# Laying out the start of a three-stage kernel part by part, and moving the second stretch of retention two dense steps later

## The chip, the cores and the metric

One core of a Trainium2 chip runs the whole program in one launch. The metric is the device time of one execution in microseconds (us); less is better. A profile is one execution of the program as the hardware profiler saw it, and times inside it count from the start of its span.

## The reference

Three stages follow each other on 2304 tokens (4 sequences of 576) of width 512:

```python
# 1 retention, 8 heads of width 64
ret = (q @ k.T) / sqrt(64) * gamma[h] ** (i - j) * (i >= j);  x = ret @ v
# 2 a dense layer pair, weights w_in (512 x 2048), w_out (2048 x 512), stored as 64-bit floats
h = x @ w_in;  g = max(h, 0) + log1p(exp(-abs(h)));  x = g @ w_out
# 3 eight experts, the two best per token, weights w1 (512 x 1024), w2 (1024 x 512) each
noisy = x @ w_gate + log1p(exp(x @ w_noise)) * noise
out[token] = sum over its 2 experts of weight * (max(x @ w1[e], 0) @ w2[e])
```

## The kernel before, in words

Values that need more than float16 are kept as a high and a low float16 part, and a product is three matmuls (high-high, high-low, low-high) into one PSUM sum.

**Retention** works on 18 chunks of 128 tokens. Per chunk c: two loads (`qk`, `kv`, 512 KB each, L208 and L212), a scaling of v (`att_scale`, L222), a first stretch on TensorE (`att_in`, L239 and L244), a mask (L246) and the state sums (L257, L259) on VectorE, a second stretch on TensorE (`att_out`, L274), a scaling by position (L282, VectorE) and the split into high (L288, ScalarE) and low (L290). Three chunks make one dense tile of 384 tokens. The tiles in PSUM called `pa` have two buffers; `att_in` takes both, and from chunk 3 on `att_out` takes both.

**The dense layers** go over 6 tiles of 384 tokens by 16 blocks of 128 hidden units. A step `g1(t, f)` is 12 matmuls of 384 columns (L301), then ScalarE and VectorE work on pairs of blocks: Relu and Abs (L310, L311), Exp and Ln (L313, L314), the sum (L315), its high part (L316) and low part (L318). A step `g2(t, f)` is 9 matmuls of 512 columns (L332) and needs the pair that holds block f. The second layer runs four or five steps behind the first.

**The dense weights** arrive as 64-bit floats, 1 MB a piece, 16 pieces, through a ring of 4 buffers. A piece is scaled (L144, ScalarE), and per half its low bits are taken out (L155, ScalarE) and joined with the rest (L156 and L158, VectorE); then its high part (L164, ScalarE) and low part (L165, GpSimd) are made. After the last piece the same buffers take the expert weights, which 64 times are loaded (L347, L349), split (L356 ScalarE, L357 VectorE) and stored as float16 (L361).

**Experts** follow after the dense layers (L678, L706): they begin near 390 us and are not touched.

**What sets the order.** Until the list `order` of dense steps takes over, a string `START` names the parts in the order in which they are traced: `A` load a chunk, `S` scale, `Q` first stretch, `V` second stretch with all that follows, `L`, `a`, `b` load, decode and split a piece, `g` the next dense step, `W` warming matmuls. The scheduler of the framework then arranges every engine's queue itself from this order, and may put later instructions ahead where it thinks an engine free. From chunk 7 on, `at(...)` binds a chunk's parts to dense steps. All loads and stores are issued by SyncE in one queue, in its order; four special transfers are in it too: the routing table, the noise, two small gate weights (L385 to L389), and a write of zeros over the whole 4608 KB output (`out_zero`, L376), which is bound to dense step 44 but has no input to wait for.

Of the kernel before, what the change touches and what calls it, by code (L numbers as in the profile page):

```python
# [10 lines left out]
F32 = mybir.dt.float32  # L11
# [11 lines left out]
P = 128  # L23
C = 128
# [60 lines left out]
def body(ctx, tc, ins, out):  # L85
# [44 lines left out]
    def decode_load(src):  # L130
        d = ring("d64", 0, 0, [1024], I64, 4)
        nc.sync.dma_start(out=d.rearrange("p (a b) -> p a b", a=src.shape[1]), in_=src)
        return d

    def decode(d, k):

        w = d.bitcast(I32).rearrange("p (n t) -> p n t", t=2)
        u = d.bitcast(U16).rearrange("p (n t) -> p n t", t=4)  # L140
        h = d.bitcast(F32).rearrange("p (n t) -> p n t", t=2)[:, :, 1]
        f = ring("df", 1, 0, [1024], F32, 3)
        A = f.bitcast(I32)
        nc.scalar.activation(h, h, AF.Copy, scale=2.0 ** -111)  # L144


        for n in range(2):
            r = slice(n * 512, (n + 1) * 512)
            if n and k < 5:
                low = ps.tile([P, 512], I32, tag="p2", name="low", bufs=3)  # L150
            elif n and k > 6:
                low = ps1.tile([P, 512], I32, tag="pa", name="low", bufs=2)
            else:
                low = ps.tile([P, 512], I32, tag="sm", name="low", bufs=1)
            nc.scalar.activation(low, u[:, r, 1], AF.Copy, bias=2.0 ** -14 - 0.5, scale=2.0 ** -13)  # L155
            nc.vector.scalar_tensor_tensor(out=low, in0=w[:, r, 1], scalar=3, in1=low,  # L156
                                           op0=ALU.logical_shift_left, op1=ALU.bitwise_or)
            nc.vector.scalar_tensor_tensor(out=A[:, r], in0=w[:, r, 1], scalar=-2 ** 31, in1=low,  # L158
                                           op0=ALU.bitwise_and, op1=ALU.bitwise_or)
        return f  # L160

    def parts(f, hi, lo):
        fv = f.rearrange("p (a b) -> p a b", a=hi.shape[1])
        nc.scalar.activation(hi, fv, AF.Copy)  # L164
        nc.gpsimd.tensor_tensor(out=lo, in0=fv, in1=hi, op=ALU.subtract)  # L165

    w_in = ins["moe_w_in"].rearrange("(k p) f -> p k f", p=P)
    w_out = ins["moe_w_out"].rearrange("(c p) d -> p c d", p=P)
    DEC = {}


    PIECES = [("i", 0), ("i", 1)] + [p for i in range(6) for p in (("i", i + 2), ("o", i))] + [("o", 6), ("o", 7)]
    LOADS, DECS, PARTS = list(PIECES), list(PIECES), list(PIECES)

    def piece(what):
        if what == "L" and LOADS:
            w, i = LOADS.pop(0)
            DEC[w, i] = decode_load(w_in[:, :, i * 256:(i + 1) * 256] if w == "i" else w_out[:, 2 * i:2 * i + 2, :])
        elif what == "a" and DECS:
            n = DECS.pop(0)  # L180
            DEC[n] = decode(DEC[n], len(PIECES) - 1 - len(DECS))
        elif what == "b" and PARTS:
            w, i = PARTS.pop(0)
            f = DEC.pop((w, i))
            if w == "i":
                parts(f, wi[:, 0, :, i * 256:(i + 1) * 256], wi[:, 1, :, i * 256:(i + 1) * 256])
            else:
                parts(f, wo[0][:, 2 * i:2 * i + 2, :], wo[1][:, 2 * i:2 * i + 2, :])
# [13 lines left out]

    def kinds(c):
        return [(2 * c + x) % PAIR for x in range(2)]

    def att_load(c):
        qk = ap.tile([P, 2, 8, HALF], F32, name="qk", bufs=3)
        nc.sync.dma_start(out=qk, in_=ins["qk"][c])  # L208
        if c == 0:
            nc.sync.dma_start(out=cd, in_=ins["c_down"])  # L210
        kv = ap.tile([P, 2, 8, D], F32, name="kv", bufs=3)
        nc.sync.dma_start(out=kv, in_=ins["kv"][c])  # L212
        if c < 5:
            n = 2 * c
            m = min(n + 2, PAIR)
            nc.sync.dma_start(out=UP[:, n:m], in_=ins["c_up"][:, n:m])
        LD[c] = (qk, kv)

    def att_scale(c):
        qk, kv = LD[c]  # L220
        e = nc.vector if c < 1 else nc.gpsimd
        e.tensor_tensor(out=kv[:, 1], in0=kv[:, 1], in1=down[:, c % PAIR, :, None].to_broadcast([P, 8, D]), op=ALU.mult)  # L222

    def att_in(c, tag="pa"):

        qk, kv = LD[c]
        ka, kb = kinds(c)
        pool, n = (ps, 3) if tag == "p2" else (ps1, 2)
        pa = pool.tile([P, 8, HALF], F32, tag=tag, name="pa", bufs=n)
        pst = pool.tile([P, 8, D], F32, tag=tag, name="pst", bufs=n)  # L230
        use = (ka < PAIR - 1, kb < PAIR - 1)
        with ExitStack() as tied:
            for j in range(4):
                for r in range(2):
                    g = r * 4 + j
                    for p in range(2):
                        x = p ^ r
# [7 lines left out]
        a = AA[c] = ap.tile([P, 8, HALF], F32, name="a", bufs=2)
        nc.vector.tensor_tensor(out=a, in0=pa, in1=tri[:, None, :].to_broadcast([P, 8, HALF]), op=ALU.mult)  # L246
        sa = ST.get(2 * c)
        for x in range(2):
            if not use[x]:
                continue  # L250
            st = ST[2 * c + x + 1] = ring(("st", x), 1, 21504 + x * 2048, [4, D], F32, 2)
            old = ST.get(2 * c + x)
            for r in range(2):
                y = ROW[1 - r ^ x]
                add = pst[y, 4 * x:4 * x + 4]
                if (ka, kb)[x] == 0:
                    nc.vector.tensor_copy(st[y], add)  # L257
                else:
                    nc.vector.tensor_tensor(out=st[y], in0=old[ROW[r ^ x]], in1=add, op=ALU.add)  # L259

    def att_out(c, tag="pa"):
# [7 lines left out]
        with ExitStack() as tied:  # L269
            both = parts + mine if kk[1] else mine + parts  # L270
            end = {(x, r): n for n, (i, j, x, r) in enumerate(both)}
            for n, (inter, j, x, r) in enumerate(both):
# [16 lines left out]
        e = nc.vector if c < 3 else nc.gpsimd
        e.tensor_tensor(out=lo, in0=f, in1=hi, op=ALU.subtract)  # L290
# [452 lines left out]
    def at(g, f, *a):  # L743
        todo.setdefault(g, []).append((f, a))
# [179 lines left out]
```

## Time and profile before

| | us |
|---|---|
| three runs | 918.84, 920.08, 920.14 (median 920.08) |
| the profiled execution: time / span | 919.36 / 917.5 |
| busy in it: TensorE / VectorE / ScalarE / GpSimd | 878.6 / 668.8 / 383.7 / 256.1 |

How to read it: PE is TensorE's matmuls, DVE VectorE, ACT ScalarE, POOL GpSimd, SP SyncE, whose queue is SPq. The share of busy time is a mean over stages: the first 125 us, the dense stage up to about 390 us and the experts after it have different limits. The profiled time is 0.72 us under the median of the runs.

### The profile page before, as it was taken

What the parts mean: (1) busy time and instruction counts of PE and PEld (TensorE: products, weight loads), DVE (VectorE), ACT (ScalarE), POOL (GpSimd) and SP (SyncE); (2) the same over time, 40 slices, a digit from 0 to 9 for tenths busy, and PEclk for the clock granted to TensorE, in tenths of its full rate; (3) what the DMA queues carried; (4) which work ended last, traced back from release to release, by engine and by line L of the source; (5) the groups of instructions that cost most, each with busy time, mean ns of one, the idle gap of its engine ahead of it and who ended that gap; (6) DMA issues with size and microseconds to landing.
All of it is one profiled execution on the core that took longest, in us unless ns stands there. A gap on an engine that the chain in (4) does not pass through costs nothing. (4 is left out here: it accounts for less than half of the span.)

```text
span 917.5 us, 19458 instructions
## 1 busy us (share of the span) xinstructions
PE 878.6 (96%) x6458; PEld 450.7 (49%) x6458; DVE 668.8 (73%) x1402; ACT 383.7 (42%) x595; POOL 256.1 (28%) x232
## 2 busy tenths in 40 slices
PE   7878999999999999899999999999999999999996
PEld 6544555555455555455544444444444444444442
DVE  5678977797787976334636789878888788887880
ACT  3679966675666674335431122221122212222120
POOL 2366642511311120200412422322223222321112
PEclk8789999999999999999999999999999999999999
DMA  9867999999999994002277664866357746866412
GB/s 349 310 241 224 337 306 406 333 326 371 353 354 330 347 374 102 2 1 69 63 243 141 123 123 82 253 167 173 71 152 174 196 136 163 244 172 162 116 24 34
DMA packets 141103, 186.88 MB, mean 204 GB/s; under 512 B 79888, under 2 KB 89360, under 8 KB 138960
## 3 DMA queue, kind: packets, MB, share of 16 engines
q1 hardware_dynamic: 130512, 164.56, 55.5%
q0 software_dynamic: 10496, 21.05, 11.8%
q8 instruction: 60, 0.98, 0.4%
q14 instruction: 35, 0.29, 0.1%
HBM read 245.67 MB, written 54.20 MB: 327 GB/s over the span
## 5 line engine op out<-in xcount | busy, mean ns | idle before, releaser
L697 DVE STREAM_TRANSPOSE ht<-hr 32x256 f32<-32x256 f32 x608 | 265.1, 436 | 11.7
L678 PE MATMUL ph<-w,xt 128*128 x984 | 220.6, 381 | 2.0 <-DMA xt<-xr 2.0
L706 PE MATMUL py<-w,ht 128*128 x984 | 218.6, 379 | 0.0
L332 PE MATMUL p<-w,g 128*128 128x512 f16 x864 | 204.9, 384 | 7.7 <-POOL w L165 5.3
L301 PE MATMUL pg<-x,wi 128*128 128x384 f16 x1152 | 204.7, 328 | 1.8 <-ACT x L288 1.3
L678 PEld LDWEIGHTS <-xt 128*128 128x128 f16 x984 | 96.5, 98 | 119.0 <-issue 2.2
L301 PEld LDWEIGHTS <-wi 128*128 128x128 f16 x1152 | 111.9, 98 | 85.6 <-issue 2.9
L706 PEld LDWEIGHTS <-ht 128*128 128x128 f16 x984 | 96.3, 98 | 116.1
L718 POOL DMA_INDIRECT out_dram<-y,ti x41 | 64.9, 1583 | 282.0 <-ACT y L717 256.5
L332 PEld LDWEIGHTS <-g 128*128 128x128 f16 x864 | 83.2, 99 | 99.8 <-issue 11.5
L683 ACT ACTIVATE hr<-ph 128x512 f16<-128x512 f32 x82 | 60.1, 733 | 159.3 <-PE ph L678 156.2
L357 DVE SCALAR_TENSOR_TENSOR w<-w 128x1024 f16<-128x1024 f32 x64 | 83.8, 1320 | 36.7 <-ACT w L356 31.2
L684 DVE SCALAR_TENSOR_TENSOR hr<-ph,hr 128x512 f16<-128x512 f32 x82 | 59.4, 728 | 67.7 <-ACT hr L683 66.0
L717 ACT ACTIVATE y<-py,ti 128x512 f32<-128x512 f32 x41 | 28.2, 687 | 180.4 <-PE py L706 175.9
L356 ACT ACTIVATE w<-w 128x1024 f16<-128x1024 f32 x64 | 67.4, 1054 | 62.4 <-DMA w<-in_moe_w_dram 39.3
L315 DVE SCALAR_TENSOR_TENSOR r<-a,r 128x768 f32<-128x768 f32 x48 | 54.7, 1140 | 50.7 <-ACT a L314 50.0
L510 POOL DMA_INDIRECT table<-tb,pos x36 | 40.8, 1135 | 140.3 <-DVE pos L495 100.4
L310 ACT ACTIVATE r<-pg 128x384 f32<-128x384 f32 x96 | 46.3, 482 | 73.9 <-PE pg L301 72.3
L290 POOL TENSOR_TENSOR x<-w,x 128x512 f16<-128x512 f32 x15 | 20.8, 1385 | 116.6 <-ACT x L288 73.9
L655 POOL DMA_INDIRECT xr<-X,ti x41 | 43.4, 1057 | 18.8 <-POOL ti L652 10.4
L311 ACT ACTIVATE a<-pg 128x384 f32<-128x384 f32 x96 | 46.5, 484 | 0.0
L313 ACT ACTIVATE a<-a 128x768 f32<-128x768 f32 x48 | 40.4, 842 | 1.1
(129 smaller groups left out, 649.1 us busy)
## 6 DMA issues: line engine op xcount, KB each, us to landing
w<-wsc SPq DMA_DIRECT2D x78, 2048.0 KB
w<-in_moe_w_dram SPq DMA_DIRECT2D x64, 512.0 KB
wsc<-w SPq DMA_DIRECT2D x64, 512.0 KB
qk<-in_qk_dram SPq DMA_DIRECT2D x18, 512.0 KB
kv<-in_kv_dram SPq DMA_DIRECT2D x18, 512.0 KB
w<-in_moe_w_in_dram SPq DMA_DIRECT2D x8, 1024.0 KB
w<-in_moe_w_out_dram SPq DMA_DIRECT2D x8, 1024.0 KB
out_dram<-zero SPq DMA_DIRECT2D x1, 4608.0 KB
```

The costliest lines, as they stand in the source:

```text
L301: nc.tensor.matmul(pg, lhsT=wi[:, a, k, f * P:(f + 1) * P], rhs=x[:, b, k, :], start=n == 0, stop=n == 11)
L311: nc.scalar.activation(a[:, i], pg, AF.Abs)
L315: nc.vector.scalar_tensor_tensor(out=r, in0=a, scalar=S_G, in1=r, op0=ALU.mult, op1=ALU.add)
L332: m = nc.tensor.matmul(PG[t, j], lhsT=g[:, a, f % 2, j * P:(j + 1) * P], rhs=wo[b][:, f, :], start=f == 0 and a + b == 0, stop=f == NFB - ...
L356: nc.scalar.activation(h[:, 0], t, AF.Copy, scale=s)
L357: nc.vector.scalar_tensor_tensor(out=h[:, 1], in0=t, scalar=s, in1=h[:, 0], op0=ALU.mult, op1=ALU.subtract)
L678: M1[i].append(nc.tensor.matmul(ph, lhsT=xt[:, a * 4 + k, :], rhs=AR[0][:, ds(r * 8192 + (b * 4096 + k * 1024 + n * 512), 512)], start=m = ...
L683: LAST["act"] = nc.scalar.activation(hi, ph, AF.Relu)
L684: nc.vector.scalar_tensor_tensor(out=lo, in0=ph, scalar=0.0, in1=hi, op0=ALU.max, op1=ALU.subtract)
L697: nc.vector.transpose(dst[32 * f:32 * f + 32, :, t], src[32 * t:32 * t + 32, :, f])
L706: M2[i].append(nc.tensor.matmul(py, lhsT=ht[:, c, :, a], rhs=AR[1][:, ds(r * 8192 + (b * 4096 + c * 512), 512)], start=len(M2[i]) == 0, st ...
L718: LAST["pool"] = nc.gpsimd.indirect_dma_start(out=out[:, :], out_offset=bass.IndirectOffsetOnAxis(ap=ti[:, 1:2], axis=0), in_=y[:, :], in_ ...
```

## The change

1. The work up to the end of the first dense tile is cut into smaller parts (a load, a scaling, half a decoded piece, a mask, one state sum, one Relu and Abs, and so on), 230 of them, and a new string names them in the order that TensorE, ScalarE, VectorE, GpSimd and SyncE have to keep among these parts. A letter behind a number gives the engine (`a` ScalarE, `v` VectorE, `g` GpSimd) or, for `l` and `k`, the PSUM tile.
2. The work of a part moves between engines: of the scalings of pieces (`h`, 16 of 1024 columns in size, two of them as halves) 8 go from ScalarE to GpSimd; of the high parts (`p`) 6 go to GpSimd and 4 to VectorE; of the low parts (`q`) 5 go to VectorE; of the high parts of g (`C`) 3 go to ScalarE and 3 to GpSimd.
3. The first piece of w_in is cut in two halves, which makes 17 pieces on the ring of 4, so piece 16 now lies in the buffer of piece 0. The first weights come first, and `kv` before `qk`.
4. Chunk 6 leaves the string and is bound to dense steps like the later ones; the second stretch of every chunk from 6 on comes 4 dense steps behind the first instead of 2; state sums are issued behind the mask.
5. `route_load` and what follows in `order` are outside the fixed part: the scheduler still places them.

```diff
-    PIECES = [("i", 0), ("i", 1)] + [p for i in range(6) for p in (("i", i + 2), ("o", i))] + [("o", 6), ("o", 7)]
+    PIECES = [("i", 0, 1), ("i", 1, 1), ("i", 2, 2)]
+    PIECES += [p for f in range(0, 12, 2) for p in (("i", f + 4, 2), ("o", f, 2))] + [("o", 12, 2), ("o", 14, 2)]
...
+    def piece_scale(n, e="a"):
...
+        if e == "a":
+            nc.scalar.activation(h, h, AF.Copy, scale=2.0 ** -111)
+        else:
+            ENG[e].tensor_scalar(h, h, 2.0 ** -111, None, op0=ALU.mult)
...
+    def piece_word(n, r):
+        if r == 0:
+            DEC[n] = ring("df", 1, 0, [1024], F32, 3)
...
+    def piece_hi(n, e="a"):
+        v, hi, lo = piece_parts(n)
+        copy(e, hi, v)
+
+    def piece_lo(n, e="g"):
+        v, hi, lo = piece_parts(n)
+        ENG[e].tensor_tensor(out=lo, in0=v, in1=hi, op=ALU.subtract)
...
     def att_load(c):
+        kv = ap.tile([P, 2, 8, D], F32, name="kv", bufs=3)
+        nc.sync.dma_start(out=kv, in_=ins["kv"][c])
+        if c == 0:
+            nc.sync.dma_start(out=cd, in_=ins["c_down"])
         qk = ap.tile([P, 2, 8, HALF], F32, name="qk", bufs=3)
         nc.sync.dma_start(out=qk, in_=ins["qk"][c])
-        if c == 0:
-            nc.sync.dma_start(out=cd, in_=ins["c_down"])
-        kv = ap.tile([P, 2, 8, D], F32, name="kv", bufs=3)
-        nc.sync.dma_start(out=kv, in_=ins["kv"][c])
...
+    def att_first(c):
+        att_in(c)
+        with tie(att_mask(c)):
+            att_state(c, 0)
+            att_state(c, 1)
+
+    def att_second(c):
+        att_out(c)
+        att_up(c)
+        att_hi(c)
+        att_lo(c)
...
-    for c in range(7, NCH):
-        g0 = max({7: 22, 8: 27}.get(c, 0), (c // 3 - 1) * NS + (-1, 4, 9)[c % 3])
-        at((1, max(12, g0 - 8)), att_load, c)
+    for c in range(6, NCH):
+        g0 = max({6: 17, 7: 22, 8: 27}.get(c, 0), (c // 3 - 1) * NS + (-1, 4, 9)[c % 3])
+        if c > 6:
+            at((1, max(16, g0 - 8)), att_load, c)
         at((1, max(16, g0 - 4)), att_scale, c)
-        at((1, g0), att_in, c)
-        at((1, g0 + 2), att_out, c)
+        at((1, g0), att_first, c)
+        at((1, g0 + 4), att_second, c)
...
+        L0 A0 h0a l0w L1 d0 A1 S0v p0v Q0 q0v l1s h1g B0 T0 B1 M0 A2 Y0 V0 S1g d1 Q1 U0 L2 p1g q1g M1 H0 T1 S2g
...
+        q16v H5 R15 O5g O4v E7 e15 D7 p15a C7v Z7v q15v D6 C6a Z6g A6
...
+    warm(20)
+    ET = mybir.EngineType
+    with tc.manual_schedule(engines={ET.PE, ET.Activation, ET.DVE, ET.Pool, ET.SP}):
+        FIXED.append(True)
+        for s in START:
+            DO[s[0]](int(s[1:].rstrip("avgspw")), *s[1:].lstrip("0123456789"))
+        FIXED.clear()
+    route_load()
+    order = [u for u in order if u[1] >= (NFB, DONE)[u[0] - 1]]
```

In the changed kernel the lines of old and new read so: L156, L158 became L169, L171; L165 became L185; L282 became L289; L246 became L249; L315 became L347; L356, L357 became L400, L401; L376 became L420; L132 became L146; L140 is a copy on any engine.

**SyncE's queue, at the last pieces of the dense weights.** Before: the pieces (L132), chunk 6 (L208, L212), the first four expert weights (L347), and behind them the zeros.

```order
L388 DMA wg_97<-in_moe_w_gate_dram 128x4x8
L389 DMA wg_97<-in_moe_w_noise_dram 128x4x8
L132 DMA w_84<-in_moe_w_out_dram 128x2x512
L208 DMA qk<-in_qk_dram 128x1024
L132 DMA w_84<-in_moe_w_out_dram 128x2x512
L212 DMA kv<-in_kv_dram 128x1024
L347 DMA w_84<-in_moe_w_dram 128x1024 x4
L376 DMA out_dram<-zero 9216x1x128
```

With the change:

```order
L432 DMA wg_97<-in_moe_w_gate_dram 128x4x8
L433 DMA wg_97<-in_moe_w_noise_dram 128x4x8
L420 DMA out_dram<-zero 9216x1x128
L146 DMA w_84<-in_moe_w_in_dram 128x4x256
L146 DMA w_84<-in_moe_w_out_dram 128x2x512
L219 DMA w_85<-in_c_up_dram 128x256
L210 DMA kv<-in_kv_dram 128x1024
L214 DMA qk<-in_qk_dram 128x1024
L146 DMA w_84<-in_moe_w_out_dram 128x2x512 x2
```

The zeros moved ahead of pieces 13 to 16 and of chunk 5.

**VectorE, where the last pieces are decoded.** Before, the last halves (L156, L158), then the first expert splits (L357) among retention and the sums of dense pairs (L315):

```order
L156 SCALAR_TENSOR_TENSOR low<-w_84,low 128x512
L391 SCALAR_TENSOR_TENSOR wg<-wg_97,wg 128x64
L158 SCALAR_TENSOR_TENSOR w_85<-w_84,low 128x512
L282 TENSOR_TENSOR w_85<-px,w_85 128x4x64
L357 SCALAR_TENSOR_TENSOR w_84<-w_84 128x1024
L282 TENSOR_TENSOR w_85<-px,w_85 128x4x64
L357 SCALAR_TENSOR_TENSOR w_84<-w_84 128x1024
L315 SCALAR_TENSOR_TENSOR r<-a,r 128x768
```

With the change, from the second word of piece 16 on (its high part, then an expert split, chunk 5's scaling by position, the low part of piece 16, chunk 4's low part, piece 15's second half between two splits, and dense pair 7):

```order
L171 SCALAR_TENSOR_TENSOR w_85<-w_84,low 128x512
L140 CAST w_84<-w_85 128x1024
L401 SCALAR_TENSOR_TENSOR w_84<-w_84 128x1024
L289 TENSOR_TENSOR w_85<-px,w_85 128x4x64 x2
L185 TENSOR_TENSOR w_85<-w_85,w_84 128x1024
L303 TENSOR_TENSOR x_757<-w_85,x_757 128x4x128
L169 SCALAR_TENSOR_TENSOR low<-w_84,low 128x512
L401 SCALAR_TENSOR_TENSOR w_84<-w_84 128x1024
L171 SCALAR_TENSOR_TENSOR w_85<-w_84,low 128x512
L401 SCALAR_TENSOR_TENSOR w_84<-w_84 128x1024
L347 SCALAR_TENSOR_TENSOR r<-a,r 128x768
L140 CAST g<-r 128x768
```

Behind these follow one more split, pair 7's low part, piece 15's low part, and only then pair 6's sum (L347).

**VectorE around chunk 8.** Before: mask (L246), states (L257, L259), scaling by position (L282).

```order
L246 TENSOR_TENSOR a<-pa,w_85 128x512
L315 SCALAR_TENSOR_TENSOR r<-a,r 128x768
L257 COPY w_85<-pst 64x256
L316 CAST g<-r 128x768
L257 COPY w_85<-pst 64x256
L318 TENSOR_TENSOR g<-r,g 128x768
L259 TENSOR_TENSOR w_85<-w_85,pst 64x256 x2
L357 SCALAR_TENSOR_TENSOR w_84<-w_84 128x1024 x3
L282 TENSOR_TENSOR w_85<-px,w_85 128x4x64 x2
```

With the change, the scaling by position of chunk 8 (L289) is followed at once by the mask and states of chunk 9 (L249, L259, L261):

```order
L289 TENSOR_TENSOR w_85<-px,w_85 128x4x64 x2
L347 SCALAR_TENSOR_TENSOR r<-a,r 128x768
L140 CAST g<-r 128x768
L401 SCALAR_TENSOR_TENSOR w_84<-w_84 128x1024
L355 TENSOR_TENSOR g<-r,g 128x768
L249 TENSOR_TENSOR a<-pa,w_85 128x512
L259 COPY w_85<-pst 64x256 x2
L261 TENSOR_TENSOR w_85<-w_85,pst 64x256 x2
```

On TensorE six matmuls of the second layer now stand between the second stretch of chunk 8 and the first stretch of chunk 9; before, two steps of the first dense layer and two of the second stood there.

## Rows read from the trace of the kernel before

**Rows 1.** Windows: stretch in us, busy time of each engine (instructions), TensorE's granted clock, DMA share, GB/s.

```profile
75.00:100.00 25.00, 22.14 (x152) 11.09 (x153) 20.45 (x26) 23.29 (x37) 16.09 (x9) 1.00 0.81 265
...
125.00:350.00 225.00, 218.73 (x2242) 121.96 (x2240) 178.58 (x300) 150.98 (x235) 51.99 (x40) 0.99 0.97 343
...
450.00:900.00 450.00, 447.99 (x2121) 204.72 (x2119) 349.38 (x819) 99.04 (x145) 119.60 (x129) 1.00 0.61 152
```

**Rows 2.** Timeline of TensorE, the second layer's steps 12 and 13: start, duration, line.

```profile
113.82 2.10 PE L332 MATMUL p<-w,g 128*128 128x512 f16 x9
115.76 2.11 PE L301 MATMUL pg<-x,wi 128*128 128x384 f16 x12
```

**Rows 3.** Groups by line and form, 0 to 122 us: busy us, mean ns | idle before.

```profile
L156 DVE SCALAR_TENSOR_TENSOR low<-w,low 128x512 int32<-128x512 int32 x32 | 21.6, 690 | 9.3 <-ACT low L155 9.3
L158 DVE SCALAR_TENSOR_TENSOR w<-w,low 128x512 int32<-128x512 int32 x32 | 21.5, 684 | 1.0
...
L165 POOL TENSOR_TENSOR wi<-w,wi 128x1024 f16<-128x1024 f32 x8 | 17.8, 2229 | 12.1 <-ACT wi L164 12.1
...
L315 DVE SCALAR_TENSOR_TENSOR r<-a,r 128x768 f32<-128x768 f32 x9 | 16.4, 1822 | 6.1 <-ACT a L314 5.9
...
L259 DVE TENSOR_TENSOR w<-w,pst 64x256 f32<-64x256 f32 x22 | 8.9, 419 | 0.9 <-PE pa L244 0.3
...
L313 ACT ACTIVATE a<-a 128x768 f32<-128x768 f32 x9 | 7.6, 845 | 0.1
...
L282 DVE TENSOR_TENSOR w<-px,w 128x256 f32<-128x256 f32 x14 | 5.5, 418 | 3.5 <-PE px L274 3.5
...
L500 DVE COPY tb<-tok 128x6 int32<-128x6 int32 x6 | 0.9, 153 | 0.0
...
L222 DVE TENSOR_TENSOR kv<-kv,w 128x512 f32<-128x512 f32 x1 | 0.7, 693 | 6.3 <-DMA kv<-in_kv_dram 6.3
```

**Rows 4.** Timeline of VectorE: sum and high part of dense pairs, an expert split.

```profile
93.28 2.25 DVE L315 SCALAR_TENSOR_TENSOR r<-a,r 128x768 f32<-128x768 f32 x1 [0.95 <-ACT a L314]
...
96.06 0.55 DVE L316 CAST g<-r 128x768 f16<-128x768 f32 x1
...
103.75 0.96 DVE L315 SCALAR_TENSOR_TENSOR r<-a,r 128x768 f32<-128x768 f32 x1
...
117.69 1.21 DVE L357 SCALAR_TENSOR_TENSOR w<-w 128x1024 f16<-128x1024 f32 x1
```

**Rows 5.** Timeline of GpSimd, 92 to 97 us: low part of a piece and of g.

```profile
92.59 2.13 POOL L165 TENSOR_TENSOR w<-w,w 128x1024 f16<-128x1024 f32 x1 [1.41 <-ACT w L164]
96.75 1.65 POOL L318 TENSOR_TENSOR g<-r,g 128x768 f16<-128x768 f32 x1 [2.03 <-DVE g L316]
```

**Rows 6.** Timeline of SyncE's queue: the gate weights and the zeros.

```profile
82.61 4.01 SPq L388 DMA_DIRECT2D wg<-in_moe_w_gate_dram  x1
...
101.62 0.56 SPq L376 DMA_DIRECT2D out_dram<-zero  x1
```

**Rows 7.** Windows behind the issue of the zeros, columns as in rows 1.

```profile
106.00:112.00 6.00, 6.00 (x85) 3.75 (x84) 5.80 (x9) 5.42 (x8) 3.74 (x2) 1.00 1.15 346
112.00:118.00 6.00, 6.00 (x35) 3.30 (x34) 6.00 (x5) 4.30 (x8) 4.68 (x2) 1.00 1.15 347
118.00:122.00 4.00, 4.00 (x24) 2.15 (x23) 3.88 (x4) 2.47 (x4) 2.48 (x1) 1.00 1.09 393
```

**Rows 8.** Waits, 0 to 140 us: who waited for whom, total us, times, longest.

```profile
ACT w L356 <- DMA w<-in_moe_w_dram: 4.8, 1, 4.8
```

**Rows 9.** The page's costliest groups: the expert split on ScalarE, columns as in rows 3.

```profile
L356 ACT ACTIVATE w<-w 128x1024 f16<-128x1024 f32 x64 | 67.4, 1054 | 62.4 <-DMA w<-in_moe_w_dram 39.3
```

**Rows 10.** Waits of TensorE, 125 to 420 us.

```profile
PE px L274 <- DVE w L259: 5.9, 5, 2.0
```

**Rows 11.** Timeline of TensorE: end of a second stretch; a second-layer step behind a wait.

```profile
211.70 0.65 PE L274 MATMUL px<-a,kv 64*64 64x64 f32 x32
...
237.82 3.77 PE L332 MATMUL p<-w,g 128*128 128x512 f16 x9
```

**Rows 12.** Timeline of VectorE: the scaling by position behind the stretch that ended at 212.35.

```profile
218.67 0.76 DVE L282 TENSOR_TENSOR w<-px,w 128x256 f32<-128x256 f32 x2
```

More of the change, by code (lines that the diff above doesn't have):

```diff
@@ L128, in body @@
     wo = [view(a, 32768, [NFB, DM], F16) for a in range(2)]
[L130 to L160, printed above, removed]
@@ L175, in piece @@
[L175 to L188, printed above, removed]
+    ENG = {"a": nc.scalar, "v": nc.vector, "g": nc.gpsimd}
@@ L190, in warm, with piece_parts @@
+    def piece_parts(n):
+        w, f, m = PIECES[n]
+        hi, lo = (wi[:, b, :, f * P:(f + m) * P] if w == "i" else wo[b][:, f:f + m, :] for b in range(2))
+        return DEC[n][:, :m * 512].rearrange("p (a b) -> p a b", a=hi.shape[1]), hi, lo
+    def piece_hi(n, e="a"):
[4 more added lines that the diff above has]
+        ENG[e].tensor_tensor(out=lo, in0=v, in1=hi, op=ALU.subtract)
     def warm(n):
@@ L242, in att_in, with att_mask, att_state, att_out @@
                                 LAST["in"] = c
-                                tied.enter_context(tc.issue_after(m.ins))
+                                tied.enter_context(tie(m))
                         nc.tensor.matmul(pa[ROW[p], g], lhsT=qk[ROW[p], 1, g], rhs=qk[ROW[p], 0, g], start=True, stop=True)
[L245 to L261, printed above, removed]
-        (qk, kv), a = LD.pop(c), AA.pop(c)
-        pool, m = (ps, 3) if tag == "p2" else (ps1, 2)
-        px = [pool.tile([P, 4, HALF], F32, tag=tag, name="px", bufs=m) for x in range(2)]
+    def att_mask(c):
+        pa = AA[c]
+        AA[c] = ap.tile([P, 8, HALF], F32, name="a", bufs=2)
+        return nc.vector.tensor_tensor(out=AA[c], in0=pa, in1=tri[:, None, :].to_broadcast([P, 8, HALF]), op=ALU.mult)
+    def att_state(c, x):
+        pst, k = ST["sum", c], kinds(c)[x]
+        if k == PAIR - 1:
+            return
+        new = ST[2 * c + x + 1] = ring(("st", x), 1, 21504 + x * 2048, [4, D], F32, 2)
+        for r in range(2):
+            y, z = ROW[1 - r ^ x], ROW[r ^ x]
+            if k == 0:
+                nc.vector.tensor_copy(new[y], pst[y, 4 * x:4 * x + 4])
+            else:
+                nc.vector.tensor_tensor(out=new[y], in0=ST[2 * c + x][z], in1=pst[y, 4 * x:4 * x + 4], op=ALU.add)
+    def att_out(c):
+        (qk, kv), a = LD.pop(c), AA.pop(c)
+        if c < 3:
+            px = [ps.tile([P, 4, HALF], F32, tag="p2", name="px", bufs=3) for x in range(2)]
+        else:
+            px = [ps1.tile([P, 4, HALF], F32, tag="pa", name="px", bufs=2) for x in range(2)]
+        AA["out", c] = px
         kk = kinds(c)
```

156 lines of the change are left out of this document (95 added, 61 removed).

## The prediction

> **What bounds the kernel now.** I read the windows first. From 450 us on TensorE works 448.0 of 450 us [rows 1]: the experts are its own time, and the change does not reach them. From 125 to 350 us it works 218.7 of 225, so at most 6 us lie there for waits, and the waits of TensorE name nearly all of it: the second stretch of retention waits 5.9 us in five places for state sums on VectorE [rows 10]. The start is different. From 75 to 100 us ScalarE is busy 23.3 of 25 us while TensorE has only 22.1 and VectorE 20.5 [rows 1]: decoding the dense weights on ScalarE sets the pace, and TensorE takes each dense step when its weights come. So the change has two places to act: the start, up to where TensorE is fed without a gap, and the five waits.
>
> To compare starts I need one mark. Step 12 of the second dense layer begins at 113.8 us [rows 2], and from there TensorE runs on. In the changed order steps 17 and 18 of the first layer and a quarter of step 19 stand ahead of that step (at 1.95 us each, from the starts in [rows 2], 4.4 us), and chunk 6's second stretch, which before was ahead of it, comes later (two halves of 0.65, some 1.3 us [rows 11]). The same progress is thus worth 113.8 + 4.4 - 1.3 = **116.9 us**. If the changed kernel starts that step at T, the start gains 116.9 - T.
>
> **The start, by VectorE's queue.** ScalarE loses eight scalings and half of the high parts, so I take VectorE as the next bound and add its written order. Up to the last word of piece 8 stand: 16 halves at 0.690 + 0.684 (22.0), 16 state sums at 0.419 (6.7), 8 scalings by position at 0.418 (3.3) [rows 3], 5 masks taken like a word, 0.69 (3.4), a scaling of v 0.69 and two low parts of that size (2.1) [rows 3], 3 sums at 0.96 (2.9) and 3 casts at 0.55 to 0.73 (1.8) [rows 4], twelve copies at 0.153 and seven smaller constants (2.4) [rows 3]: 44.6 us. Its first word cannot come much before 6.5 us: in the old kernel the first loaded chunk kept VectorE waiting 6.3 us [rows 3], and half a piece is less to load. Piece 8 is then done at 6.5 + 44.6 = 51 us, if VectorE never waits.
>
> Now the queue of transfers. When piece 8's buffer is free, SyncE issues piece 12, then noise and gate weights (one of them held it 4.0 us [rows 6]), then the zeros, and only behind them pieces 13 and 14, chunk 5, pieces 15 and 16. In the old kernel the zeros were issued at 101.6 us [rows 6], and the windows show what they do: 12 us at a flat 346 GB/s and share 1.15, then 393 [rows 7]. 4608 KB at 346 GB/s are 13.6 us; with the flat rate through all of it I take it that what is queued behind gets nothing meanwhile. From 51: issue at 56, piece 12 and the small loads ahead on the engines to 59, zeros to 72. Pieces 13 and 14, the last position factors and chunk 5's kv are 2.65 MB, at 393 GB/s 7 us: 79. VectorE asks for that kv (it scales chunk 5 itself) after 2 state sums, 8 halves, 2 sums, a cast, two low parts of the size of a split at 1.21 [rows 4]: 0.8 + 11 + 1.9 + 0.7 + 2.4, with 2.5 for GpSimd (below), 19 us after 51, at 70. It **waits 9 us** there. Then 0.7 + 7 halves (9.6) + scaling by position, sum, mask, 4 state sums (4.2) + 0.5: the last word of piece 16 at 94, where the old kernel had its last word at about 109.5.
>
> **What then stands in the way.** Piece 16 lies in the buffer that the first expert weights take, so their load waits for that last word. Behind the word in VectorE's queue stands the split of just these weights, and behind the split all that the next dense steps need. The load: 0.4 issue, 1.3 for 512 KB, the rest the delay of a transfer; 4 us in all, near the one such wait in the old trace, 4.8 [rows 8]. ScalarE's half 1.05 [rows 9], the split 1.2 [rows 4]: 100.3. Scaling by position 0.8, a low part 1.2, another 0.7, half a piece, a split, half a piece: 107. The third expert's ScalarE half needs that half piece (1.05, to 108); Exp and Ln of pair 7 stand behind it on ScalarE (2 x 0.845 [rows 3], 109.7); then on VectorE sum and high part 1.5; the fourth split waits for two more ScalarE operations (113); low part 1.0, piece 15's low part 1.2, and at last pair 6's sum (1.0): 116.2. High part on ScalarE 0.8, low part on GpSimd 1.65 [rows 5]. **T = 118.6 us.** Behind it I see nothing that stops TensorE again. The start costs 118.6 - 116.9 = +1.7 us: ScalarE's relief is real (the last word is 15 us earlier), and is given back at the zeros and at this tail.
>
> **GpSimd, scalings and high parts.** The trace has no such operation on GpSimd. Below is VectorE's cast, 0.73 for 1024 columns from 0.55 for 768 [rows 4]; above, GpSimd's own low part of the same size, 2.2 with two inputs [rows 3]. I take 1.1, half of that for half the inputs. GpSimd has 11.5 low parts of pieces (25.6), 7 of g (11.6), 4 chunks each scaled and split (some 9), 13 scalings and high parts and 3 casts (16.7): 63 us, less than VectorE. At 2.2 it is 79. The Trainium skill (GPSIMD Engine Reference, Engine selection) calls one-input work there roughly line rate; 1024 columns at the 1.2 GHz it states would be an estimate of 0.85 us and GpSimd's sum 59; no row here shows it.
>
> A sum of a pair took 0.96 us with GpSimd idle and 2.25 when it began inside a GpSimd low part [rows 4, 5]: it began at 93.28, GpSimd ended at 94.72, and 0.81 later it was done. The means say the same, 1.82 over nine [rows 3]. That is where my 2.5 us come from: five such meetings at 0.5.
>
> **The second stretch, two steps later.** Two steps are 7.8 us more for the state sums. All five waits go (-5.9). One of them also let the granted clock fall: the nine matmuls at 237.8 took 3.77 instead of 2.10 us [rows 2, 11] (-1.7). Against it: first and second stretch share two PSUM buffers, and the next chunk's first stretch now comes 0.7 to 2 steps behind instead of 2 to 3. It waits for the scaling by position, and in the old kernel that ended at 219.4, 7 us after a stretch that ended at 212.35 [rows 11, 12]; others I read were at 1 to 5 us. Over ten such pairs, most with 4 to 6 us between, I put 2.5 us. Chunk 8's second stretch now comes right ahead of tile 2, whose first step needs that chunk's low part: 3 us of other work lie between, scaling, high and low part need at least 0.8 + 0.6 + 1.2: 0 at the least, 7 if VectorE is as late as there; I put 2.5. Together -2.6. The bounds are -7.6 and +5.
>
> **Sum.** The profiled execution took 919.4; 919.4 + 1.7 - 2.6 = 918.5. It is 0.7 under the median of the runs, so for a median I say **919.0 us**. What a measurement of this kernel can tell from no change is about 0.2%, 1.8 us.
>
> **Rivals.**
> 1. *The zeros and the tail do not bind.* The loads are early enough, or chunk 5 arrives in time, and the first split finds its weights. For it: the waits of 9 and 4 us are each a difference of long sums. Without both T is some 107, the gain 10: **908 us**.
> 2. *GpSimd and VectorE hold each other up (slower).* VectorE's operations with two SBUF inputs add 25 us (8 sums 7.7, low parts and scalings 9, casts 4, four splits 4.8) to GpSimd's 63. If they exclude each other fully, the pair has 88 us of work from 8 us on, at 2.2 us for the new operations 104. It decides once those cost over 1.5 us: then pair 6's low part on GpSimd ends 8 us later than I have it, **927 us**. The rule that would make it so is the Trainium skill's (SBUF — State Buffer, Who interferes with whom): a two-input VectorE instruction and a GpSimd one that reads SBUF lock each other out for a whole instruction; the meeting at 93.28 agrees, and ScalarE's work moved to GpSimd then buys less than it frees.
> 3. *The later stretch only changes what it waits for.* Five waits go, but the shared buffers and tile 2's first step cost as much: no gain there, **922 us**.
>
> **Chances.** Own forecast 0.43 (own range 914 to 923; faster 0.16, same 0.15, slower 0.12), rival 1 0.24, all faster; rival 2 0.21, all slower; rival 3 0.12 (same 0.04, slower 0.08). Faster 0.40, same 0.19, slower 0.41. A range of 908 to 930 leaves out about 2 in 10.
>
> **What the changed profile would show.** Right: the last decoded word near 94 us; a wait of VectorE for kv of chunk 5 near 70 to 79; the zeros as a flat stretch of 13 us in the DMA windows before 75; ScalarE waiting some 3 us for expert weights; step 12 of the second layer near 119; no wait of the second stretch for state sums behind 125 us. Wrong: if kv is there when asked for; if GpSimd is never idle between 50 and 110 us; if the first stretch waits for the scaling by position by over 6 us in sum.

## The result and the profile after

| | us |
|---|---|
| four runs of the changed kernel | 926.64, 929.85, 930.40, 933.33 (median 930.12) |
| four runs of the kernel before beside them | median 919.46 |
| ratio | 1.0118, 95% interval 1.0078 to 1.0157 |
| profiled execution: time / span | 929.85 / 928.0 |
| busy in it: TensorE / VectorE / ScalarE / GpSimd | 878.7 / 672.8 / 372.2 / 268.9 |

The change made the kernel 1.2% slower, some 10.7 us. A second measurement (run e14) gave 1.0154. Later runs were made on several chips, on which the kernel before took 910 to 918 us; so ratios to it are compared, not times.

The windows of the changed kernel, columns as in [rows 1]:

```profile
6.09:57.84 51.75, 38.69 (x665) 26.08 (x665) 43.94 (x90) 29.60 (x48) 42.01 (x25) 0.79 0.89 325
66.00:78.00 12.00, 12.00 (x67) 6.31 (x65) 11.05 (x14) 7.35 (x13) 7.05 (x4) 1.00 1.15 348
75.00:90.00 15.00, 7.22 (x78) 3.51 (x75) 6.72 (x10) 6.30 (x11) 6.96 (x4) 0.80 1.07 394
118.00:125.00 7.00, 4.93 (x16) 2.31 (x16) 6.89 (x10) 5.68 (x9) 1.64 (x1) 0.52 1.04 392
125.00:350.00 225.00, 211.58 (x2153) 116.87 (x2154) 170.61 (x290) 141.57 (x220) 49.15 (x36) 0.98 0.95 330
```

Set them beside [rows 1]. (The dense layers last longer than is said ahead of the prediction: near 390 us it is retention that ends, and the first expert matmul starts at 478.6 us in the kernel before, at 492.9 in the changed one.) From 125 to 350 us TensorE works 7 us less than it did. And there is a hole that was not there: from 75 to 90 us it works 7.22 of 15 us, and VectorE, ScalarE and GpSimd are no busier, while the transfers are full. What it looks like on SyncE's queue, on VectorE and on TensorE:

```profile
63.54 1.63 SPq L420 DMA_DIRECT2D out_dram<-zero  x1
65.67 11.34 SPq L146 DMA_DIRECT2D w<-in_moe_w_in_dram  x1
...
78.28 0.37 SPq L210 DMA_DIRECT2D kv<-in_kv_dram  x1
```

```profile
57.15 0.69 DVE L171 SCALAR_TENSOR_TENSOR w<-w,low 128x512 int32<-128x512 int32 x1
...
77.71 1.23 DVE L185 TENSOR_TENSOR w<-w,w 128x1024 f16<-128x1024 f32 x1
87.11 1.24 DVE L223 TENSOR_TENSOR kv<-kv,w 128x512 f32<-128x512 f32 x1 [8.18 <-DMA kv<-in_kv_dram]
...
105.37 0.69 DVE L171 SCALAR_TENSOR_TENSOR w<-w,low 128x512 int32<-128x512 int32 x1
```

```profile
120.06 4.96 PE L326 MATMUL pg<-x,wi 128*128 128x384 f16 x15 [3.73 <-ACT a L338]
124.82 4.19 PE L376 MATMUL p<-w,g 128*128 128x512 f16 x18
```

The zeros are issued at 63.5 us. The issue of piece 13 behind them alone takes SyncE 11.3 us, and chunk 5's kv comes 8.2 us after VectorE asks for it. The last word of piece 16 ends at 106.1 (half of piece 15 follows it, to 114.5), and step 12 of the second layer starts at 124.8. The mark for the same progress was 116.9, so **the start lost 7.9 us**; the spans differ by 10.5, so 2.6 were lost behind it. Near the end of the start TensorE waits 3.7 us for Abs, and the granted clock of 118 to 125 us is 0.52, near the lower of its two levels (1.2 of 2.4 GHz): the 15 matmuls at 120.06 take 4.96 us, where [rows 2] have 12 in 2.11, which would make 2.6.

The 2.6 us behind the start are a net figure. From step 12 to the first expert matmul, and from there to the end, the windows are, before (two lines) and changed (two lines):

```profile
113.82:478.60 364.78, 355.14 (x3244) 195.37 (x3243) 247.48 (x479) 211.78 (x346) 80.78 (x68) 0.99 0.72 250
478.60:917.50 438.90, 428.08 (x2012) 194.05 (x2010) 336.07 (x769) 89.31 (x127) 117.01 (x120) 0.99 0.60 143
...
124.82:492.85 368.03, 354.61 (x3281) 194.38 (x3280) 240.88 (x480) 206.43 (x337) 72.40 (x62) 0.99 0.68 232
492.85:928.00 435.15, 426.38 (x2012) 193.66 (x2010) 335.79 (x769) 89.32 (x127) 116.66 (x120) 1.00 0.61 144
```

The dense part is 3.2 us longer, although by the mark 3.1 us less of it are left there: some 6.3 us lost. The experts are 3.8 us shorter with the same matmuls; TensorE stands idle 8.8 us there instead of 10.8.

The waits of TensorE from 125 to 420 us, beside the 5.9 us of [rows 10]:

```profile
PE pst L239 <- DVE w L289: 5.0, 3, 2.5
PE px L279 <- issue: 2.4, 6, 0.4
PE pg L326 <- ACT a L338: 2.4, 2, 2.1
PE pst L239 <- issue: 2.1, 1, 2.1
PE pg L326 <- POOL x L303: 1.5, 1, 1.5
```

All waits of the second stretch for state sums are gone. In their place first stretches wait for the scaling by position. One of the three, on VectorE, behind a second stretch that ended at 164.5:

```profile
164.44 1.22 DVE L401 SCALAR_TENSOR_TENSOR w<-w 128x1024 f16<-128x1024 f32 x1 [0.52 <-ACT w L400]
166.04 0.96 DVE L347 SCALAR_TENSOR_TENSOR r<-a,r 128x768 f32<-128x768 f32 x1 [0.38 <-ACT a L343]
167.03 0.56 DVE L140 CAST g<-r 128x768 f16<-128x768 f32 x1
167.63 0.96 DVE L355 TENSOR_TENSOR g<-r,g 128x768 f16<-128x768 f32 x1
168.50 1.22 DVE L401 SCALAR_TENSOR_TENSOR w<-w 128x1024 f16<-128x1024 f32 x1
169.64 0.75 DVE L289 TENSOR_TENSOR w<-px,w 128x256 f32<-128x256 f32 x2
```

and on TensorE:

```profile
163.86 0.65 PE L279 MATMUL px<-a,kv 64*64 64x64 f32 x32
...
170.11 0.33 PE L239 MATMUL pst<-kv 64*64 64x64 f32 x2 [1.45 <-DVE w L289]
```

Five operations stand ahead of the scaling (L289); it starts 5.1 us after the stretch that it reads. Only one step of each layer, 3.9 us, lies between this stretch and the next chunk's first one, which needs the buffers.

GpSimd's groups up to 125 us, columns as in [rows 3]: a scaling of a piece takes 3.04 us, a cast of the same size 1.16.

```profile
L156 POOL TENSOR_SCALAR w<-w 128x1024 f32<-128x1024 f32 x7 | 21.3, 3041 | 12.8 <-DMA w<-in_moe_w_in_dram 12.8
...
L140 POOL CAST w<-w 128x1024 f16<-128x1024 f32 x3 | 3.5, 1164 | 0.0
```

### The profile page after: what moved, and what is told of

Its sections match the earlier page's. It is cut to its first block, busy times and chain, and to the rows that moved or that the text cites. A ratio compares the mean times of both kernels' runs of the same rounds, so it can differ in the third digit from the quotient of the medians.

```text
span 928.0 us, 19445 instructions
## 1 busy us (share of the span) xinstructions
PE 878.7 (95%) x6454; PEld 447.3 (48%) x6454; DVE 672.8 (73%) x1410; ACT 372.2 (40%) x582; POOL 268.9 (29%) x240
## 5 line engine op out<-in xcount | busy, mean ns | idle before, releaser
L326 PE MATMUL pg<-x,wi 128*128 128x384 f16 x1152 | 210.6, 335 | 19.9 <-ACT a L338 6.1
L376 PE MATMUL p<-w,g 128*128 128x512 f16 x864 | 205.2, 386 | 3.5 <-POOL w L185 1.8
L326 PEld LDWEIGHTS <-wi 128*128 128x128 f16 x1152 | 114.2, 100 | 109.4 <-issue 21.0
L376 PEld LDWEIGHTS <-g 128*128 128x128 f16 x864 | 83.3, 99 | 98.3 <-issue 10.3
L401 DVE SCALAR_TENSOR_TENSOR w<-w 128x1024 f16<-128x1024 f32 x64 | 81.3, 1275 | 36.6 <-ACT w L400 36.2
L347 DVE SCALAR_TENSOR_TENSOR r<-a,r 128x768 f32<-128x768 f32 x48 | 49.2, 1025 | 53.3 <-ACT a L343 53.1
L400 ACT ACTIVATE w<-w 128x1024 f16<-128x1024 f32 x64 | 67.4, 1054 | 50.0 <-DMA wsc<-w 32.2
L355 DVE TENSOR_TENSOR g<-r,g 128x768 f16<-128x768 f32 x41 | 40.3, 984 | 0.9
```

The source lines that it names most:

```text
L326: nc.tensor.matmul(pg, lhsT=wi[:, a, k, f * P:(f + 1) * P], rhs=x[:, b, k, :], start=n == 0, stop=n == 11)
L347: nc.vector.scalar_tensor_tensor(out=r, in0=PG.pop(("a", i)), scalar=S_G, in1=r, op0=ALU.mult, op1=ALU.add)
L376: m = nc.tensor.matmul(PG[t, j], lhsT=g[:, a, f % 2, j * P:(j + 1) * P], rhs=wo[b][:, f, :], start=f == 0 and a + b == 0, stop=f == NFB - ...
L400: nc.scalar.activation(h[:, 0], t, AF.Copy, scale=s)
L401: nc.vector.scalar_tensor_tensor(out=h[:, 1], in0=t, scalar=s, in1=h[:, 0], op0=ALU.mult, op1=ALU.subtract)
```

## The experiments

Three suspects: GpSimd's price, the place of the zeros, the later second stretch. Each was first undone by itself.

**e1: scalings back on ScalarE.**

```diff
-        L0 A0 h0a l0w L1 d0 A1 S0v p0v Q0 q0v l1s h1g B0 T0 B1 M0 A2 Y0 V0 S1g d1 Q1 U0 L2 p1g q1g M1 H0 T1 S2g
-        Y1 V1 B2 O0v L3 Q2 U1 l2w h2g M2 H1 T2 k2s L4 O1g d2 V2 U2 l3p h3g e2 A3 H2 k3w O2g d3 p2a G0 h4a q2g L5
+        L0 A0 h0a l0w L1 d0 A1 S0v p0v Q0 q0v l1s h1a B0 T0 B1 M0 A2 Y0 V0 S1g d1 Q1 U0 L2 p1g q1g M1 H0 T1 S2g
+        Y1 V1 B2 O0v L3 Q2 U1 l2w h2a M2 H1 T2 k2s L4 O1g d2 V2 U2 l3p h3a e2 A3 H2 k3w O2g d3 p2a G0 h4a q2g L5
...
```

> The changed kernel with the eight scalings of pieces that it had given to GpSimd back on ScalarE, at the same places of the written order; all else as in the change. Theory G (GpSimd's price: a scaling takes 2.96 us there where I had put 1.1, GpSimd is full from 22 to 73 us, and VectorE waits for it): the second word of piece 8 is done near 51 us instead of 57.8, the zeros go out near 57, chunk 5's kv comes near 79, the last word near 98, step 12 of the second layer starts near 117 to 119 instead of 124.8; 6 to 8 us less than the change, 922 to 924. Theory Z (the zeros alone decide, whenever they come): piece 8 gets earlier, but VectorE waits the longer for kv, and the time falls by under 3 us, 927 or more. Theory E (VectorE and GpSimd lock each other out and the sum of both counts): GpSimd's 23 us less shorten VectorE's operations too, and more than 8 us are gained, under 921.

Measured: 1.0104 (1.0073 to 1.0135), 0.14% below the change's first measurement and 0.5% below its second (e14): 1 to 5 us, and the intervals overlap both times, so it may be nothing. Theory G fell at its first number, the second word of piece 8 in this run:

```profile
57.88 0.69 DVE L171 SCALAR_TENSOR_TENSOR w<-w,low 128x512 int32<-128x512 int32 x1
```

It ends at 58.6, no earlier than in the change, although GpSimd lost its 3 us operations. E fell too: taking eight long GpSimd operations away from beside VectorE gave no 8 us. Z is what is left, though its piece 8 was to come earlier too, and by the ratio alone the gain may be over its 3 us.

**e2: zeros behind the last store of expert weights.**

```diff
+    def late_zero():
+        with behind("store"):
+            out_zero()
...
-    at((2, 44), out_zero)
+    at((2, 82), late_zero)
```

> The changed kernel with the write of zeros moved in SyncE's queue behind the last store of expert weights (near 350 us); all else as in the change. Theory Z: the waits for piece 13 (GpSimd 9.9, ScalarE 8.0) and for chunk 5's kv (VectorE 8.2) shrink to under 2 us, and step 12 of the second layer starts near 116 to 118; 7 to 8 us less than the change, 922 to 923. Theory T (the tail behind the last word decides: one split after the other and the loads they need): the last word comes 8 us earlier, but the expert weights load only 3 us earlier, and under 4 us are gained, 926 or more. Both: nothing is lost at 350 us, where the DMA share is 0.2.

Measured: 1.0022 (1.0000 to 1.0044), so 1.0% to 1.3% less than the change. VectorE takes chunk 5's kv without a wait, and step 12 starts 10.9 us earlier. Six matmuls of the first layer (some 1.0 us) moved behind it, so 9.9 us are like for like, and the mark, 115.9 then, is beaten by 2.0:

```profile
80.73 2.62 DVE L223 TENSOR_TENSOR kv<-kv,w 128x512 f32<-128x512 f32 x1
```

```profile
111.07 3.04 PE L326 MATMUL pg<-x,wi 128*128 128x384 f16 x9 [3.58 <-ACT a L338]
113.90 4.21 PE L376 MATMUL p<-w,g 128*128 128x512 f16 x18
```

Theory Z holds, with more gained than its 7 to 8 us, and T falls: the tail let the whole gain through. **The place of the zeros is the largest part of the loss.**

**e3 and e4: the number of steps.** Two steps in the changed kernel (first pair of lines), four in the old one (second pair):

```diff
-        at((1, g0 + 4), att_second, c)
+        at((1, g0 + 2), att_second, c)
...
-        at((1, g0 + 2), att_out, c)
+        at((1, g0 + 4), att_out, c)
```

> The changed kernel with the second stretch of retention two dense steps behind the first again instead of four, for all chunks from 6 on; the written order as in the change. Theory S (the later stretch only exchanges waits: five waits for state sums, 5.9 us in the old kernel, against three waits of a first stretch for the scaling by position, 5.0 us, and one of 1.5 for a low part): the old waits come back and the new ones go; within 2 us of the change, 928 to 932. Theory L (the later stretch is worse): 2 to 4 us less, 926 to 928. My forecast's own step (the later stretch gains 2.6): 2 to 4 us more, 932 to 934.

> The kernel before with one number changed: the second stretch of chunks 7 to 17 four dense steps behind the first instead of two. Theory S: within 2 us of the kernel before, 918 to 922, with the waits for state sums gone and waits of first stretches for the scaling by position in their place. Theory L: 2 to 4 us slower, 922 to 924. The forecast's step: 2.6 us faster, 917.

Measured: e3 1.0072 (1.0045 to 1.0099), e4 1.0055 (1.0033 to 1.0077). The later stretch costs 0.5 to 0.8%, some 4 to 7 us, in both kernels: theory L, and rather more than it said. (In the changed kernel the difference is clear of noise only against e14.) The waits in the two profiles trade as theory S had it, and e4's profiled execution was the fastest of its twelve, so they did not settle where the loss lies; see e13.

**e5 and e9: zeros elsewhere in the old kernel**: in e5 by the edit of e2, in e9 behind the last store of the fifth tile's rows.

```diff
+    def late_zero():
+        with tc.issue_after(STORE[4, 2].ins):
+            out_zero()
...
-    at((2, 44), out_zero)
+    at((2, 81), late_zero)
```

> The kernel before with its write of zeros moved behind the last store of expert weights, as in the run with late zeros. Theory P (it is the place ahead of pieces 13 to 16 that costs, not the zeros): in the old kernel they came behind the last piece, and only the first expert weights waited (4.8 us of ScalarE, which TensorE did not feel); within 2 us of the kernel before. Theory Q (13 us of exclusive transfer cost wherever they lie ahead of 350 us, since the transfers are busy to 0.97 of the time from 125 to 350): 5 to 10 us faster than before.

> The kernel before with the zeros behind the last stores of the fifth tile's rows, where the transfers are idle for some 50 us (share 0.01 to 0.03 from 360 to 410 us). Theory C (behind the last store of expert weights the zeros had collided with the transposes of the fifth tile's rows, one of which took 7.5 us there, and that is why late zeros made the kernel before 0.4% slower): the transposes take 1.3 us each, and the time is that of the kernel before or up to 0.3% less. Theory D (no collision; the zeros had held something at 101 us that is better held, or the difference lies elsewhere): again 0.3 to 0.5% slower.

Measured: e5 1.0042 (1.0019 to 1.0066): both theories missed, the place at 340 us is worse than the old one. e9 0.9973 (0.9955 to 0.9992): theory C. SyncE's queue in e5, then in e9, shows the first transpose behind the zeros, and without them:

```profile
338.37 0.60 SPq L376 DMA_DIRECT2D out_dram<-zero  x1
345.76 7.52 SPq L420 DMA_TRANSPOSE w<-w  x1
```

```profile
345.75 1.24 SPq L420 DMA_TRANSPOSE w<-w  x1
```

So e2's gain is no gift of the late place as such; late zeros can cost by themselves. How e5 lost its 0.4% is not shown: its profiled execution was the fastest of its twelve (908.42 us), and in it TensorE waits 0.7 us for a transpose.

**e6, e7, e8: late zeros and two steps together**, then with ScalarE's scalings, then (e8, from e6) with VectorE's halves of the expert splits queued behind pair 6's sum; e8's edit:

```diff
-        nc.vector.scalar_tensor_tensor(out=h[:, 1], in0=t, scalar=s, in1=h[:, 0], op0=ALU.mult, op1=ALU.subtract)
+        with behind("sum6"):
+            nc.vector.scalar_tensor_tensor(out=h[:, 1], in0=t, scalar=s, in1=h[:, 0], op0=ALU.mult, op1=ALU.subtract)
```

> The changed kernel with both: zeros behind the last store of expert weights, and the second stretch two steps behind again. Theory A (the two losses are separate): ratios add up, 1.0022 less 0.0046, so 0.9976 of the kernel before, 2 us faster. Theory B (what the early stretch saves is hidden once the zeros are gone): as with late zeros alone, 1.0022.

> As the run before it, and the eight scalings back on ScalarE. Theory G2 (the zeros had hidden GpSimd's 2.96 us a scaling; without them it decides): 4 to 8 us faster than that run. Theory H (VectorE's own queue sets the pace to piece 12 either way, and GpSimd's price is covered): within 2 us of that run.

> As the run with late zeros and two steps, and VectorE's halves of the expert splits queued behind pair 6's sum, out of the tail of the written order. Theory T (the splits in the tail hold up pairs 6 and 7, Relu and Abs behind them, and TensorE, 3.6 us in one place plus a fallen clock): the wait of TensorE for Abs goes, step 12 of the second layer starts 4 to 6 us earlier, 3 to 6 us faster than that run. Theory U (the splits' stores and the next loads come later by as much, and with the transfers busy to 0.97 the expert weights are what is late): no gain, within 2 us, or slower.

Measured: e6 1.0000 (0.9982 to 1.0019), between A and B, and it decides for neither. e7 **0.9944 (0.9920 to 0.9968)**, faster than both kernels: theory G2. With the zeros out of the way GpSimd's price does show, 0.56%, 5 us. Step 12 in e6 and in e7:

```profile
112.92 3.04 PE L326 MATMUL pg<-x,wi 128*128 128x384 f16 x9 [5.06 <-ACT a L338]
115.75 2.47 PE L376 MATMUL p<-w,g 128*128 128x512 f16 x6
```

```profile
109.86 2.79 PE L326 MATMUL pg<-x,wi 128*128 128x384 f16 x9 [4.20 <-ACT a L338]
112.46 4.60 PE L376 MATMUL p<-w,g 128*128 128x512 f16 x18
```

e8 1.0060 (1.0038 to 1.0081), slower than e6: theory U. The wait for Abs shrank from 5.1 to 2.2 us and step 12 came at 112.6, but the splits' stores came later and the zeros with them, into the transposes (the queue, then a wait of TensorE in e8):

```profile
340.46 0.79 SPq L423 DMA_DIRECT2D out_dram<-zero  x1
348.24 7.86 SPq L467 DMA_TRANSPOSE w<-w  x1
```

```profile
PE lg L484 <- DMA w<-w: 2.7, 1, 2.7
```

From step 12 to the first expert matmul e8 takes 6.1 us more than e6 (364.3 against 358.2): 3.2 us more of idle time, this wait most of it, and 2.9 us of slower matmuls; behind the wait, from 360 to 375 us, the granted clock is 0.89, where e6 has 1.00.

**e10, e11, e13: two, three and four steps**, with scalings on ScalarE and the zeros behind the fifth tile's rows. Only the number in the line shown at e3 differs.

> The changed kernel with scalings on ScalarE, the second stretch two steps behind, and the zeros in the gap behind the fifth tile's rows. Theory C: as the run with late zeros, two steps and ScalarE (0.9944), or up to 0.4% less, since the zeros no more come near the transposes: 0.990 to 0.994. Theory D: 0.994 to 0.996.

> As the run before it, with the second stretch three steps behind. Theory S (two waits work against each other: too early, and the stretch waits for state sums, 4 to 6 us in all; too late, and the next first stretch waits for the scaling by position in the shared buffers, 5 us): three steps have less of both, 1 to 3 us faster than with two. Theory V (VectorE's place for the scaling, behind an expert split and a dense pair, and not the number of steps, makes the wait): within 1 us, or slower.

> The changed kernel with scalings on ScalarE and the zeros in the gap, the second stretch four steps behind as in the change: the third of a row of two, three and four steps (0.9967 and 0.9963 of the kernel before for two and three). Theory S2 (with four steps the next chunk's first stretch comes one step behind the second stretch, and VectorE, which has an expert split, a sum, a high part, a low part and one more split ahead of the scaling by position, cannot give the shared buffers back in that time): waits of first stretches for the scaling by position of 5 us or more, and 3 to 5 us slower than two or three steps: 1.000 to 1.002. Rival: the loss of four steps came with the zeros or with GpSimd's load at the start; then 0.996 to 0.998.

Measured: 0.9967 (0.9948 to 0.9986), 0.9963 (0.9944 to 0.9983) and 1.0039 (1.0020 to 1.0058). e10 met neither of its theories' gains: in e7 the zeros were issued at 328.0 already, and the first transpose, at 342.6, took 1.3 us; no collision shows there that could be removed. Between two and three steps nothing can be told. Four steps are 0.7% slower with the zeros and GpSimd's load out of it: theory S2, with a larger loss than it said. The waits of TensorE from 125 to 420 us, in e10, e11 and e13:

```profile
PE px L279 <- DVE w L261: 5.0, 5, 1.6
PE pg L326 <- ACT a L338: 1.8, 1, 1.8
```

```profile
PE pg L326 <- ACT a L338: 3.1, 3, 1.3
PE pg L326 <- POOL x L303: 1.4, 1, 1.4
```

```profile
PE pst L239 <- DVE w L289: 4.6, 2, 2.3
PE pst L239 <- issue: 4.2, 2, 2.7
```

At two steps the second stretch waits for state sums; at three nothing of either kind over 0.7 us is left; at four the first stretch waits, 4.6 us for the scaling by position (0.9 more in a row for its other product) and 4.2 with no releaser in the trace. From step 12 to the first expert matmul, e10 and e13:

```profile
112.01:469.77 357.76, 350.63 (x3287) 193.65 (x3286) 242.37 (x480) 206.36 (x338) 69.82 (x63) 0.99 0.75 252
112.07:475.98 363.91, 352.70 (x3288) 194.04 (x3287) 243.33 (x480) 206.95 (x338) 72.85 (x63) 0.99 0.74 248
```

Both start this part at the same time, and e13 needs 6.2 us more for it, near the measured difference of 0.72%, some 6.6 us: 4.1 are idle time of TensorE, 2.1 longer matmuls.

**e12: the price by itself.** Operations on 1024 numbers a partition at the start of the changed kernel; p2s is every second word of pt.

```diff
+        nc.gpsimd.tensor_scalar(p2s, p2s, 1.0, None, op0=ALU.mult)
+        nc.gpsimd.tensor_scalar(pt[:, :1024], pt[:, :1024], 1.0, None, op0=ALU.mult)
+        nc.gpsimd.tensor_copy(pt[:, 1024:], pt[:, :1024])
+        nc.gpsimd.tensor_copy(pf, pt[:, :1024])
```

> The changed kernel with twelve more operations at its start that measure prices on 128x1024 numbers: on GpSimd a scaling of every second 32-bit word in place, a scaling of adjacent words in place, a copy of adjacent words, a cast to 16 bits; on VectorE both scalings. Theory 1 (the step between words makes the scaling dear on GpSimd): 2.96 us with the step, near 1.1 without. Theory 2 (a multiplication by a constant is dear there, whatever the step): 2.9 us in both, a copy near 1.1. On VectorE both under 1.2. The time of this run says nothing.

```profile
3.47 2.91 POOL L883 TENSOR_SCALAR w<-w 128x1024 f32<-128x1024 f32 x1 [1.75 <-DVE bia L639]
6.46 2.81 POOL L884 TENSOR_SCALAR w<-w 128x1024 f32<-128x1024 f32 x1
...
11.82 1.04 POOL L885 COPY w<-w 128x1024 f32<-128x1024 f32 x1
12.82 1.04 POOL L886 CAST w<-w 128x1024 f16<-128x1024 f32 x1
```

The rows stand in the order of the edit. Theory 2: the multiplication is dear, with the step or without; copies and casts are not. VectorE scaled adjacent words in 0.69 us; with the step it took 1.53, where I expected under 1.2, beside a GpSimd operation.

**e14: the change once more**, with no edit.

> The changed kernel itself once more, for a narrower interval beside which the undone parts can be set: 1.010 to 1.014 of the kernel before. Were it under 1.008, the gain of late zeros (to 1.0022) and of two steps (to 1.0072) would have to be read as smaller.

Measured: 1.0154 (1.0121 to 1.0186), above the 1.014 that I expected at most. So the undone parts above are, if anything, sized too small against 1.0118.

## Why the prediction was wrong

I forecast 919.0 us and a range up to 930; it took 930.12. My two terms were +1.7 for the start and -2.6 behind it; the profiles have +7.9 and +2.6. (The 2.6 are what the start leaves of the difference of the spans, so that these two meet the profiled 929.85 confirms nothing.) Two steps failed: that ScalarE's relief pays for the wait behind the zeros (points 1 and 2), and the price put on the later second stretch (point 4).

1. **VectorE's queue to piece 8.** The working time was right: 44.6 us summed, 43.9 + 0.4 busy up to 57.8. The condition "if VectorE never waits" failed: beside the first load it stood idle 7.8 us (51.75 less 43.94), where I had allowed nothing, so piece 8 was done at 57.8, not 51. Its waits there were for TensorE (2.4 us), Ln on ScalarE (1.8), low bits from ScalarE (1.2) and scalings on GpSimd (1.0). It was not GpSimd's price alone that held it: e1 took that away and piece 8 stayed; but e1 gave the work to ScalarE, so no run isolates what did.
2. **The zeros.** The mechanism was right and is the main loss: an exclusive stretch (348 GB/s at a share of 1.15, as in [rows 7]), VectorE's wait for chunk 5's kv of 8.2 us against my 9. It came 8 us later than I had it, at 87.1 instead of 79, because the zeros ended near 78 us instead of 72, piece 8 being late, and the loads behind them took 9 us instead of 7. (The 11.3 us of SyncE's issue lie inside the zeros' transfer and add nothing to it.) Where I failed was the conclusion that ScalarE's relief pays for it: with the zeros late the start beats its mark by 2.0 us, with them where they are it misses it by 7.9.
3. **The tail.** Shape right, size wrong: from the last word of piece 16 to step 12 I had 24.6 us, it took 18.7. The load of the first expert weights, for which I had put 4 us, was there: ScalarE waited 0.6 us for such loads in all. The first four were issued at 89.8, 102.4, 102.8 and 106.2 us, and only the last of them behind that word. (I also counted half a piece twice, 1.4 us; the list in the change has one there.) But the word came at 106.1, not 94, so step 12 was at 124.8, not 118.6.
4. **The second stretch, -2.6.** This step failed in sign. The five waits went, as forecast, but the dense part behind the start lost some 6.3 us, and no clock was won back: the granted clock of 125 to 350 us is 0.98, before 0.99. The price of the other side, "over ten such pairs ... I put 2.5 us", was the mis-sized term: waits for the scaling by position alone were 5.0 in the change, and four steps cost 4 to 7 us net in three comparisons (e3, e4, e13 against e10). I had read the one row that showed it, a scaling 7 us behind its stretch [rows 11, 12], and took it for an outlier; with one step of each layer between, a delay over 3.9 us becomes a wait. That the net loss behind the start is only 2.6 is owed to the experts, 3.8 us shorter, which I had not forecast.
5. **GpSimd's price.** I took 1.1 us between bounds of 0.73 and 2.2. For casts that was right (1.06 to 1.16); a scaling took 3.04. My upper bound, a two-input operation, was no bound. Undone, it gave 1 to 5 us in the change (e1), not clear of noise, and 5 us with the zeros late (e7); whether by its own length or by holding up VectorE, no run separates. The Trainium skill (GPSIMD Engine Reference, Engine selection) calls one-input work roughly line rate; e12 shows 1.04 us for copies and 2.8 to 2.9 for a scaling, so for scalings the measurement decides against it.
6. **Rivals.** The first fell. The second had the sign and nearly the time (927), and the price was past the 1.5 us from which it was to decide, but its mechanism did not decide: e1 took the long GpSimd operations away and gained 0.5% at most. That its time came out near was luck. The third was right in kind (waits changed) and too mild. The wrong-side chance of 0.41 was there; what was missing is that points 1 and 4 would both go against me, which the range did not allow for.

Whether the written order itself is worth anything is not settled: e7, with it, is at 0.9944, the old kernel with only its zeros moved (e9) at 0.9973, and the intervals overlap. Nor was the move of high and low parts, the halved first piece or the order of the loads undone by itself.

## What to carry to other kernels

When a schedule is written out for the engines, look first at what the transfers' queue now holds ahead of the loads that the next operations ask for: here one large store with no input to wait for was put ahead of them, and moving it behind them was worth more than any other part that was undone. When a consumer is moved later to spare it a wait, find who waits for the buffers that it gives back, and count the steps left between. A sum of one engine's work gives the end only if you also add what it waits for on the way.

## What the runs showed of the hardware

- GpSimd multiplies 128x1024 32-bit numbers by a constant in 2.8 us (adjacent) to 2.9 us (every second), copies or casts as many in 1.04, and takes 2.1 to 2.2 for a two-input subtraction of that size; VectorE multiplied adjacent ones in 0.69.
- SyncE itself was held behind the 4.6 MB of zeros: the next issue took 11.34 us (10.9 to 12.9 in e1, e3 and e14), where most others take 0.4.
- A transpose by transfer that was issued 7.4 to 7.8 us behind the zeros took SyncE 7.5 to 7.9 us (e5, e8); one issued 14.6 to 16.6 us behind them took 1.3 (e2, e6, e7).
